# Two attention-and-mixer stages on one core: batch 2's q and k turned by DMA, w4 loaded later, work moved between engines

## The chip, the core and the metric

One core of a Trainium2 chip runs one program. The metric is device time in microseconds for one execution. Five engines work side by side, each in the order in which its instructions were written, and wait for one another through semaphores: TensorE (PE in the rows; its weight loads are PEld), VectorE (DVE), ScalarE (ACT), GpSimd (POOL) and SyncE (SP), which only issues DMA transfers. SP, POOL and ACT can each issue DMAs into a queue of their own; sixteen DMA engines serve the queues.

## The reference

For eight batches of 576 tokens with 8 heads of 64:

```python
scores = q @ k.T / 8                 # heads 0-3: keys of the last 32 tokens
attn = softmax(where(mask, scores))  # heads 4-7: every 4th key of the last 128
x = attn @ v                         # (576, 512), heads side by side
h = relu(x.T @ w_tok1) @ w_tok2      # mixes tokens
u = x + h.T
out = u + relu(u @ w_ch1) @ w_ch2    # mixes channels, 512 -> 1536 -> 512
```

Inputs and output are float32; the kernel works in float16 with float32 sums.

## The kernel before

For each batch the work has these parts, named by their tiles.
- q, k and v are loaded by SP (`emit_loads_qk`, `load_v`) and cast to float16, mostly on POOL (`cast_steps`, L275 to L286; 17 steps: the tails of q and k, then q and k of four pairs of heads, then v as four blocks `vn`, a tail `vt`, two `vd` and `vx`).
- q and k are turned, so that the 64 channels lie on partitions. For batches 0 and 1 TensorE does it against an identity (`transposes`). For batch 2 TensorE does it too (`unpad` L381, `turn_tails` L396, with copies out of PSUM on ScalarE and VectorE). For batches 3 to 7 DMA transposes issued by SP do it (`dma_steps` L348: tails, then q and k of the first two pairs, then of the last two), and POOL copies turned k into the order in which the scores read it (`place_steps` L367).
- Scores: batches 0 and 1 add the mask on TensorE as a product. Batches 2 to 7 have `scores_twin` (L509), one call for heads 0 to 3 (g = 0) and one for heads 4 to 7 (g = 1): 24 products into six PSUM banks, then six exponentials on ScalarE, then masks multiplied on POOL.
- Values (`values`), eight heads: products into a bank, then a reciprocal and a product on VectorE.
- Token mixing: `emit_h1` (rectified on VectorE or ScalarE) and `emit_u`, where u is the sum with x. For some blocks the sum is formed on TensorE by an identity product and ScalarE copies it ("summed"); for the others VectorE adds.
- u is turned (`emit_uT` by TensorE for batches 0 and 1, `uT_dma` and `uT_place` for the rest).
- Channel mixing: `gen_first` is the first layer, twelve blocks `gp` of four products with 512 columns, each rectified into `gta` (L770); for odd batches there are three more groups `gt` for the tails of two batches. `gen_second` is the second layer `yp`, which reads w4 = w_ch2; twelve products fill half an output block, and VectorE adds u.

The order of instructions is written out by `interleave` (L819): a main generator (layers of an earlier batch) yields its cost in estimated us, and steps of later batches carry a place on that scale; a step is emitted as soon as the main work has passed its place. The number is only a place in the order. The change touches the first such call, with batch 0's first layer as main work and batch 1's attention as steps (L1000 to L1005), and the second, with the first layer of batch 1 and the second layers of batches 0 and 1 as main work and the attention of batches 2 and 3 as steps (L1007 to L1024). Ahead of them stand the casts of batch 1 on POOL (L990), between which POOL issues the loads of w3's last third and of w4's three thirds.

PSUM has eight banks: three that `gp`, `gt` and `yp` take in turn ("main"), three for values, u and turning ("fl") and two for scores.

Of the kernel before, what the change touches and what calls it, by code (L numbers as in the profile page):

```python
# [69 lines left out]
def kernel(  # L70
# [201 lines left out]
    def cast_vx(b, eng):  # L272
        copy(eng, vt[b % 2][:, :, 0:64], l32[(b, "vx")])

    def cast_steps(b, eng=nc.gpsimd):  # L275
        steps = [lambda: cast_tails_qk(b, eng)]
        for hp in range(4):
            for nm in ("q", "k"):
                steps.append(lambda nm=nm, hp=hp: cast_qk(b, nm, hp, eng))
        for s in range(4):  # L280
            steps.append(lambda s=s: cast_vn(b, s, nc.gpsimd))
        steps.append(lambda: cast_tail_v(b, nc.gpsimd))
        for h in (0, 2):
            steps.append(lambda h=h: cast_vd(b, h, nc.gpsimd))
        steps.append(lambda: cast_vx(b, nc.gpsimd))
# [4 lines left out]
    gta = fixed("gt", [128, NMB, GW])  # L290
# [218 lines left out]
    def scores_twin(b, g):  # L509

        tags = (("sc", 2), ("sc", 2), ("fl", 3), ("fl", 3), ("fl", 3), ("main", 3))
        ps = [bank(*tags[i], f"sc_{b}_{g}_{i}") for i in range(6)]
        small = ps[4:6]

        def twin(hp, banks, c, keys, queries):
            for h in range(2):
                rows = slice(64 * h, 64 * h + 64)
                n = c.stop - c.start
                nc.tensor.matmul(out=banks[h][:, c], lhsT=keys(rows), rhs=queries(rows), start=True, stop=True)  # L519

        for j in range(2):
            hp = 2 * g + j
            if g == 0:
                for kb in range(3):
                    twin(hp, ps[2 * j:2 * j + 2], slice(BLK * kb, BLK * kb + BLK),
                         lambda rows: kt[hp][rows, 128 * kb:128 * kb + 128],
                         lambda rows: qta[rows, hp, :, 32 * kb:32 * kb + 40])
            else:
                for r in range(4):
                    twin(hp, ps[2 * j:2 * j + 2], slice(128 * r, 128 * r + 128),  # L530
                         lambda rows: kra[rows, hp, r], lambda rows: qta[rows, hp, r])
        for j in range(2):
            hp = 2 * g + j
            if g == 0:
                twin(hp, small, slice(256 + 128 * j, 384 + 128 * j),
                     lambda rows: kt[hp][rows, 384:512], lambda rows: qta[rows, hp, :, 96:128])
            n = 1 + g
            for x in range(n):
                c, k0 = 64 * (n * j + x), 384 + 128 * x if g else 512
                twin(hp, small, slice(c, c + 64), lambda rows: kt[hp][rows, k0:k0 + 128],  # L540
                     lambda rows: tta[rows, hp, 0:64])
        yield 0.87

        def exp(out, in_):
            nc.scalar.activation(out=out, in_=in_, func=AF.Exp, scale=0.125)  # L545

        def main(hp):
            for h in range(2):
                p = ps[2 * (hp % 2) + h]
                if g == 0:  # L550
                    exp(plain_blocks(hp)[:, h, 0:3, 0:BLK].rearrange("p b (m r) -> p b m r", r=4),
                        p[:, 0:3 * BLK].rearrange("p (b r m) -> p b m r", r=4, m=40))
                else:
                    exp(attd[hp - 2][:, h], p)

        def rest():
            for h in range(2):
                p = small[h]
                if g == 0:
                    exp(attpa[:, :, h, 3 * PST:3 * PST + 128].rearrange("p a (m r) -> p a m r", r=4),  # L560
                        p[:, 256:512].rearrange("p (a r m) -> p a m r", a=2, r=4))
                n = 1 + g
                exp(tail_cols(slice(2 * g, 2 * g + 2), g, h),
                    p[:, 0:128 * n].rearrange("p (a x c) -> p a x c", a=2, c=64))

        def mask(hp):
            if g == 0:
                w = plain_blocks(hp)[:, :, :, 0:BLK]
                mult(nc.gpsimd, w, w, band)
            else:  # L570
                w = attd[hp - 2].rearrange("p h (r c) -> p h r c", c=128)
                mult(nc.gpsimd, w, w, band[:, :, :, 0:128])
# [11 lines left out]
        mult(nc.gpsimd, t, t, tails_seen[g])  # L584
        if not g:
            mask(1)
        yield 0.0
# [30 lines left out]
    def emit_h1(b, jb, half, t):  # L618
        x = xn[b]
        j = slice(jb, DTOK, 2)  # L620
        c = slice(256 * half, 256 * half + 256)
        w = w1p if half else w1n
        p = bank("fl", 3, f"h1p_{b}_{jb}_{half}")[:, 0:256]
        nc.tensor.matmul(out=p, lhsT=w1t[b % 2][:, j], rhs=x[:, 4, c], start=True, stop=False)  # L624
        for s in range(4):
            nc.tensor.matmul(out=p, lhsT=w[:, s, j], rhs=x[:, s, c], start=False, stop=(s == 3))  # L626
        relu(nc.vector if jb and (b == 1 or (b == 0 and half)) else nc.scalar, t[:, c], p)

    def emit_u(b, s, h1):
        p = bank("fl", 3, f"up_{b}_{s}")  # L630
        if s < 4:
            summed = b == 1 and s in (0, 2)
            for half in range(2):
                c = slice(256 * half, 256 * half + 256)
                if summed:
# [110 lines left out]
    def gen_first(b):  # L746
# [17 lines left out]
        for mb in range(NMB):  # L764
            p = bank("main", 3, f"gp_{b}_{mb}")
            for i, cb in enumerate(order):
                nc.tensor.matmul(out=p, lhsT=w3_block(cb, mb), rhs=uT[(b, cb)][0], start=(i == 0), stop=(i == 3))  # L767
                if i == 1:
                    yield 0.43
            relu(nc.vector if (mb % 2 == 1 if b == 0 else mb in (1, 5)) else nc.scalar, gta[:, mb, m0:m0 + 512], p)  # L770
# [172 lines left out]
    def u_half(s, half):  # L943
        p = bank("main" if half else "fl", 3, f"up_0_{s}_{half}")[:, 0:256]
        c = slice(256 * half, 256 * half + 256)
        t = u16(0, s)[:, 2 * half:2 * half + 2]
        summed = s in (0, 2)
        if summed:
            nc.tensor.matmul(out=p, lhsT=ident, rhs=xn[0][:, s, c], start=True, stop=False)
        for jb in range(2):  # L950
# [39 lines left out]
    for i in (0, 1, 2, 3, 4, 5, 7, 6, 8, 9, 10, 11, 12, 13, 14, 15, 16):  # L990
        casts1[i]()
        if i == 1:
            load_w3(2)
        if i in (14, 15, 16):
            load_w4(next(w4s))

    def at(t0, dt, fs):
        return [(t0 + dt * i, 0.0, f) for i, f in enumerate(fs)]

    steps = score_steps(1, 0, 0, (0.0, 0.6, 0.7), (  # L1000
        (2.9, 5.0), (4.2, 6.9), (5.4, 9.3), (8.0, 12.2)))
# [69 lines left out]
```

## Time and profile before

| | us |
|---|---|
| median of three runs | 286.94 (285.69 to 287.02) |
| profiled execution | 286.81 |
| its span, first to last instruction | 285.0 |
| TensorE busy | 273.8 |
| GpSimd busy | 166.8 |
| VectorE, ScalarE busy | 132.3, 131.4 |

Times in rows count from the start of the span. A row of the timeline shows start and duration of an instruction or of a merged run of equal ones (x4), what it writes and reads, and in brackets how long its engine was idle before it and what ended that. A releaser is inferred; where several semaphores were waited for it is the last one by the profile. Matmuls overlap, so the duration of one is longer than its share of a dense run.

### The profile page before, as it was taken

Reading aid. Unit: us, or ns where it says so; the run is one execution under the profiler, and the core shown is the slowest. Engines: PE = TensorE matmul, PEld = TensorE weight load, DVE = VectorE, ACT = ScalarE, POOL = GpSimd, SP = SyncE. Lnnn points to the kernel's source line nnn. Section 1 sums busy time; section 2 is a strip of 40 time slices with the busy share of each in tenths; the row PEclk is TensorE's granted clock in tenths of the full one; section 3 lists DMA queues with packets and bytes.
Section 4 is the critical chain, followed back from the end, with each engine's and each line's share of the span. In section 5 each row is a group of like instructions: output and inputs, shape, how many; then the busy total and the mean of one; then the engine's idle time right before and its main releaser. Section 6 shows DMA issues by size and latency. Waiting matters only on the chain.

```text
span 285.0 us, 6873 instructions
## 1 busy us (share of the span) xinstructions
PE 273.8 (96%) x2760; PEld 207.0 (73%) x2760; DVE 132.3 (46%) x280; ACT 131.4 (46%) x263; POOL 166.8 (59%) x236
## 2 busy tenths in 40 slices
PE   5799899999999999999999999999999999999994
PEld 2696576676896976598776976797767966886594
DVE  6875687652365155514730263526531184322022
ACT  2964563458412374473446625482456435134500
POOL 7980853383998769769945998289945900000000
PEclk9999999999999999999999999999999999999999
DMA  7999999999658999999798989399994310521032
GB/s 217 262 227 253 269 230 241 273 223 307 165 105 191 147 332 274 190 168 352 201 191 191 319 241 188 60 235 314 207 148 83 110 39 0 111 93 37 2 86 99
DMA packets 105423, 52.60 MB, mean 185 GB/s; under 512 B 73872, under 2 KB 104208, under 8 KB 105392
## 3 DMA queue, kind: packets, MB, share of 16 engines
q1 hardware_dynamic: 101280, 47.07, 71.2%
q0 software_dynamic: 2512, 3.92, 7.6%
q10 hardware_dynamic: 1600, 1.18, 1.4%
q8 instruction: 21, 0.34, 0.5%
q14 instruction: 10, 0.08, 0.1%
HBM read 37.05 MB, written 9.44 MB: 163 GB/s over the span
## 4 chain that ended last, share of the span: by engine, by line
PE 79%; DMA 9%; POOL 4%; ACT 2%; DVE 2%; issue 1%; SPq 1%; ACTq 0%; POOLq 0%
PE gp L767 26%; PE yp L790 26%; PE h1p L626 4%; PE up L638 4%; PE gt L758 4%; PE yp L810 4%; DMA l_k<-in_k_dram 3%; DMA lt<-in_k_dram 3%; PE sc L519 2%; DMA utm<-u 2%; DMA w<-in_moe_w_tok_dram 2%; POOL attd L113 1%; PE av L605 1%; PE h1p L624 1%; PE av L600 1%
## 5 line engine op out<-in xcount | busy, mean ns | idle before, releaser
L790 PE MATMUL yp<-w,gt 128*128 128x256 f16 x756 | 86.5, 273 | 0.0
L790 PEld LDWEIGHTS <-gt 128*128 128x128 f16 x768 | 78.4, 106 | 6.2
L107 ACT ACTIVATE gt<-gp 128x512 f16<-128x512 f32 x76 | 45.4, 601 | 68.6 <-PE gp L767 68.3
L767 PE MATMUL gp<-utm,w 128*128 128x512 f16 x192 | 67.7, 379 | 0.0
L767 PE MATMUL gp<-utd,w 128*128 128x512 f16 x144 | 54.8, 380 | 0.0
L767 PEld LDWEIGHTS <-w 128*128 128x128 f16 x384 | 39.0, 114 | 20.4 <-issue 1.9
L800 DVE TENSOR_TENSOR o<-yp,u 128x512 f32<-128x512 f32 x31 | 21.4, 691 | 66.5 <-PE yp L790 64.6
L113 POOL TENSOR_TENSOR attp<-attp,const 128x1280 f16<-128x1280 f16 x12 | 31.4, 2615 | 22.4 <-ACT attp L545 18.0
L113 DVE TENSOR_TENSOR xn<-av,rec 128x320 f16<-128x320 f32 x64 | 31.5, 492 | 2.2
L113 POOL TENSOR_TENSOR attd<-attd,const 128x1024 f16<-128x1024 f16 x12 | 25.3, 2129 | 2.4 <-ACT attd L545 2.4
L644 DVE TENSOR_TENSOR u<-up,xn 128x512 f16<-128x512 f32 x26 | 17.5, 689 | 14.1 <-PE up L638 14.0
L103 POOL CAST c_k<-l_k 128x512 f16<-128x512 f32 x29 | 18.0, 623 | 8.8 <-PE tpu L675 7.6
L107 ACT ACTIVATE h<-h1p 128x256 f16<-128x256 f32 x29 | 11.1, 383 | 26.0 <-PE h1p L626 25.7
L103 POOL CAST c_q<-l_q 128x512 f16<-128x512 f32 x31 | 19.6, 635 | 2.6 <-DMA l_q<-in_q_dram 2.6
L545 ACT ACTIVATE attp<-sc 128x480 f16<-128x480 f32 (+1 forms) x36 | 16.1, 528 | 7.4 <-PE sc L519 7.4
L109 DVE TENSOR_SCALAR gt<-gp 128x512 f16<-128x512 f32 x20 | 13.7, 686 | 10.1 <-PE gp L767 10.1
L103 POOL CAST vv<-l_vn 128x256 f16<-128x256 f32 (+1 forms) x40 | 15.0, 403 | 4.0 <-DMA l_vn<-in_v_dram 3.5
L373 POOL COPY kt<-kr 128x512 f16<-128x512 f16 x10 | 10.8, 1079 | 10.4 <-DMA kr<-c_k 6.6
L697 ACT COPY utd<-utm 128x512 f16<-128x512 f16 x12 | 12.7, 1123 | 9.0 <-DMA utm<-u 9.0
L615 DVE RECIPROCAL rec<-av 128x5 f32<-128x5 f32 x64 | 12.2, 190 | 7.4 <-PE av L612 7.0
L545 ACT ACTIVATE attd<-sc 128x512 f16<-128x512 f32 x24 | 12.4, 604 | 6.1 <-PE sc L519 6.1
L758 PEld LDWEIGHTS <-w 128*128 128x128 f16 x192 | 11.9, 113 | 2.0 <-issue 0.4
(149 smaller groups left out, 441.2 us busy)
## 6 DMA issues: line engine op xcount, KB each, us to landing
out_dram<-o SPq DMA_DIRECT2D x72, 128.0 KB, 2.7
l_q<-in_q_dram SPq DMA_DIRECT2D x15, 512.0 KB, 6.9
l_k<-in_k_dram SPq DMA_DIRECT2D x14, 512.0 KB, 7.4
l_vn<-in_v_dram SPq DMA_DIRECT2D x32, 128.0 KB, 6.7
l_vd<-in_v_dram SPq DMA_DIRECT2D x16, 256.0 KB, 4.3
w<-in_moe_w_ch_dram POOLq DMA_DIRECT2D x6, 512.0 KB, 8.3
lt<-in_q_dram SPq DMA_DIRECT2D x8, 128.0 KB, 5.0
l_vt<-in_v_dram SPq DMA_DIRECT2D x8, 128.0 KB, 4.6
```

What stands on the lines that cost most here:

```text
L103: eng.tensor_copy(out=out, in_=in_)
L107: nc.scalar.activation(out=out, in_=in_, func=AF.Relu)
L109: eng.tensor_scalar_max(out=out, in0=in_, scalar1=0.0)
L113: eng.tensor_tensor(out=out, in0=x, in1=y, op=ALU.mult)
L545: nc.scalar.activation(out=out, in_=in_, func=AF.Exp, scale=0.125)
L615: nc.vector.reciprocal(out=rec[:, :, 0], in_=av[:, :, 64])
L644: nc.vector.tensor_tensor(out=u16(b, s), in0=blocks4(p), in1=blocks4(xn[b][:, s]), op=ALU.add)
L697: nc.scalar.copy(out=natural(uTd[:, cb - 2]), in_=uTm[i][:, cb].rearrange("p r m -> p m r"))
L758: nc.tensor.matmul(out=p[:, 128 * i:128 * i + 128], lhsT=w3_block(cb, 4 * g + i), rhs=uT[(b, cb)][1], start=(cb == order[0]), stop=(cb == ...
L767: nc.tensor.matmul(out=p, lhsT=w3_block(cb, mb), rhs=uT[(b, cb)][0], start=(i == 0), stop=(i == 3))
L790: nc.tensor.matmul(out=p[:, c], lhsT=gta[:, mb, a0:m0 + 512:4] if half else gta[:, mb, a0:a0 + 128], rhs=w4[mb][:, c], start=(mb == 0), st ...
L800: nc.vector.tensor_tensor(out=blocks4(o32), in0=blocks4(p), in1=u16(b, s), op=ALU.add)
```

## The change

In the first call, batch 1's scores get later places, and the turning of its q and k partly too. In the second, batch 2's q and k are turned by `dma_steps` and `place_steps` in place of `turn_steps`; its casts are emitted in two lumps, ahead of the turns and behind the placing; V of batch 2 is loaded after the turns on SP's queue; two of w4's three thirds are issued by POOL after the placing, and before the casts of V; one of these casts (the fourth `vn`) goes to ScalarE; the two twins of batch 2 stand closer together and batch 3's loads earlier. One mask of batch 2 goes from POOL to VectorE. Batch 1's h1 and part of batch 0's are rectified on ScalarE. Batch 0's first layer has one block of twelve on VectorE in place of six; the later batches have three (1, 7, 9) in place of two (1, 5). For batch 0 the u block 3 is now summed on TensorE, for batch 1 the block 0 no longer is.

```diff
-        if i in (14, 15, 16):
+        if i in (14,):
             load_w4(next(w4s))
...
-    steps = score_steps(1, 0, 0, (0.0, 0.6, 0.7), ((2.9, 5.0), (4.2, 6.9), (5.4, 9.3), (8.0, 12.2)))
+    steps = score_steps(1, 0, 0, (0.0, 0.6, 1.5), ((2.9, 5.8), (5.0, 7.7), (6.6, 9.3), (8.0, 11.4)))
-    steps += mix_steps(1, 16.0, 17.0, 18.0, 22.6, 0.6)
+    steps += mix_steps(1, 16.0, 17.0, 18.0, 30.6, 0.0)
...
-    steps = at(0, 0.0, [lambda: emit_loads_qk(2)]) + at(1.0, 0.0, [lambda: load_v(2)])
-    casts = cast_steps(2)
-    steps += at(0, 0.9, casts[:9]) + at(5.8, 0.1, casts[9:])
-    steps += turn_steps(2, (5.0, 4.8, 4.2, 6.0, 8.0, 10.3, 9.2, 12.5, 7.9, 7.0), (...))
-    steps += score_steps(2, 10.5, 4.6)
-    va = value_steps(2, 19.5, 1.2)
-    steps += mix_steps(2, 25.5, 29.0, 29.0, 37.0)
-    steps += at(13.0, 0.0, [lambda: emit_loads_qk(3)]) + at(18.0, 0.0, [lambda: load_v(3)])
-    steps += at(18.2, 0, cast_steps(3)) + at(23.0, 0.6, dma_steps(3)) + at(27.0, 0.5, place_steps(3))
-    steps += score_steps(3, 35.5, 7.0) + at(33.4, 1.5, load_steps(4))
+    steps = at(0.0, 1.5, [lambda: emit_loads_qk(2)]) + at(5.0, 6.5, [lambda: load_v(2)])
+    casts = cast_steps(2, (POOL, POOL, POOL, POOL, POOL, POOL, POOL, POOL, POOL, POOL, POOL, POOL, ACT, POOL, POOL, POOL, POOL))
+    steps += at(0.6, 0.0, casts[:9]) + at(6.5, 0.0, casts[9:])
+    steps += at(5.2, 2.5, [lambda: load_w4(next(w4s))]) + at(5.3, 1.5, [lambda: load_w4(next(w4s))])
+    steps += at(2.0, 0.5, dma_steps(2)) + at(5.1, 0.0, place_steps(2))
+    steps += score_steps(2, 10.0, 2.6)
+    va = value_steps(2, 19.0, 1.2)
+    steps += mix_steps(2, 26.6, 29.1, 30.1, 42.5)
+    steps += at(7.0, 8.0, [lambda: emit_loads_qk(3)]) + at(15.5, 0.0, [lambda: load_v(3)])
+    steps += at(17.7, 0, cast_steps(3)) + at(21.5, 1.5, dma_steps(3)) + at(27.0, 0.5, place_steps(3))
+    steps += score_steps(3, 35.0, 5.5) + at(33.4, 1.5, load_steps(4))
...
-                mult(nc.gpsimd, w, w, band)
+                mult((POOL, DVE)[hp] if b == 2 else POOL, w, w, band)
-        relu(nc.vector if jb and (b == 1 or (b == 0 and half)) else nc.scalar, t[:, c], p)
+        relu(nc.vector if jb and (b < 0) else nc.scalar, t[:, c], p)
-            relu(nc.vector if (mb % 2 == 1 if b == 0 else mb in (1, 5)) else nc.scalar, ...)
+            relu(nc.vector if mb in ((1,), (1, 7, 9), (1, 7, 9))[min(b, 2)] else nc.scalar, ...)
-            summed = b == 1 and s in (0, 2)
+            summed = b == 1 and s in (2,)
-        summed = s in (0, 2)
+        summed = s in (0, 2, 3)
```

## Rows read from the trace of the kernel before

**Rows 1.** The page: busy us of each engine, and TensorE's slices.
```profile
PE 273.8 (96%) x2760; PEld 207.0 (73%) x2760; DVE 132.3 (46%) x280; ACT 131.4 (46%) x263; POOL 166.8 (59%) x236
...
PE   5799899999999999999999999999999999999994
```
**Rows 2.** Table of stretches: busy us and instructions of each engine, clock, DMA.
```profile
30.00:40.00 10.00, 9.29 (x110) 7.06 (x111) 8.14 (x17) 6.33 (x14) 6.89 (x15) 1.00 1.21 252
```
**Rows 3.** Chain of waits, 54 to 73: start, us, what.
```profile
63.83 0.45 PE tp_q L385 x8
64.28 0.86 PE gp L767 x4
...
70.59 0.67 PE sc L519 x24
...
72.25 0.76 PE yp L790 x7
```
**Rows 4.** Groups by line and shape: busy us, mean ns of one, idle before.
```profile
L103 POOL CAST c_k<-l_k 128x512 f16<-128x512 f32 x29 | 18.0, 623 | 8.8 <-PE tpu L675 7.6 <-DMA l_k<-in_k_dram 1.1
...
L385 PE MATMUL tp_k<-const,c_k 128*128 128x128 f16 x16 | 1.5, 219 | 0.0
```
**Rows 5.** Timeline of TensorE, 28.9 to 35.2, three of its stops.
```profile
30.09 0.40 PE L310 MATMUL tp_q<-const,c_q 128*128 128x128 f16 x4 [0.50 <-POOL c_q L103]
...
32.16 0.40 PE L310 MATMUL tp_q<-const,c_q 128*128 128x128 f16 x4 [0.16 <-POOL c_q L103]
...
34.98 0.38 PE L310 MATMUL tp_k<-const,c_k 128*128 128x128 f16 x4 [0.26 <-DVE kt L103]
```
**Rows 6.** Timeline of ScalarE, one rectification.
```profile
65.18 0.60 ACT L107 ACTIVATE gt<-gp 128x512 f16<-128x512 f32 x1 [0.46 <-PE gp L767]
```
**Rows 7.** Timeline of TensorE, 54.5 to 70: stage start, twin, two stops.
```profile
54.62 3.71 PE L767 MATMUL gp<-uT,w 128*128 128x512 f16 x16
...
65.30 0.59 PE L519 MATMUL sc<-qt,kt 64*128 64x160 f16 x12
66.08 0.23 PE L519 MATMUL sc<-qt,kt 64*128 64x128 f16 x2 [0.20 <-DVE kt L103]
...
68.67 1.05 PE L758 MATMUL gt<-uT,w 128*128 128x128 f16 x16 [0.18 <-ACT attt L545]
```
**Rows 8.** DMA queues (packets, MB, share): q0 at 41 to 46, both 46 to 52, q1 65 to 69.
```profile
q0 software_dynamic: 66, 0.27, 30.4%
...
q0 software_dynamic: 286, 1.05, 86.6%
q1 hardware_dynamic: 313, 0.32, 18.5%
...
q1 hardware_dynamic: 1392, 1.37, 106.2%
```
**Rows 9.** Issue to landing: batch 2's k; w4; a block of batch 2's V at 55.
```profile
DMA to landing us min/median/max: 13.6/14.3/15.0
...
DMA to landing us min/median/max: 8.2/9.8/11.8
...
DMA to landing us min/median/max: 5.8/5.8/5.8
```
**Rows 10.** Timeline of POOL, 20 to 110: first w4 issue, one mask.
```profile
41.33 0.54 POOL L984 DMA_DIRECT2D w<-in_moe_w_ch_dram  x1 [0.19 <-issue]
...
68.54 2.60 POOL L113 TENSOR_TENSOR attp<-attp,const 128x1280 f16<-128x1280 f16 x1 [4.33 <-PE gp L767]
```
**Rows 11.** Tile kr, 83 to 93: batch 3's turns, placing, landing (min/median/max).
```profile
L351 SPq DMA_TRANSPOSE kr<-c_k x2: 1231/1248/1266, 83.9 to 87.7; - x2
L373 POOL COPY kt<-kr x2: 1055/1060/1064, 88.6 to 89.9; 128x512 f16<-128x512 f16 x2
L376 POOL COPY kt<-kr x2: 396/404/412, 91.3 to 91.6; 128x128 f16<-128x128 f16 x2
...
DMA to landing us min/median/max: 3.1/3.2/3.2
```

More of the change, by code (lines that the diff above doesn't have):

```diff
@@ L84 @@
     ps = ctx.enter_context(tc.tile_pool(name="ps", bufs=1, space=bass.MemoryType.PSUM))
+    DVE, ACT, POOL = nc.vector, nc.scalar, nc.gpsimd
     SRC = {"q": q, "k": k, "v": v}
@@ L273, in cast_vx, with cast_steps @@
         copy(eng, vt[b % 2][:, :, 0:64], l32[(b, "vx")])
-    def cast_steps(b, eng=nc.gpsimd):
-        steps = [lambda: cast_tails_qk(b, eng)]
+    def cast_steps(b, engs=(nc.gpsimd,) * 17):
+        steps = [lambda: cast_tails_qk(b, engs[0])]
         for hp in range(4):
             for nm in ("q", "k"):
-                steps.append(lambda nm=nm, hp=hp: cast_qk(b, nm, hp, eng))
+                steps.append(lambda nm=nm, hp=hp: cast_qk(b, nm, hp, engs[2 * hp + 1 + (nm == "k")]))
         for s in range(4):
[L281 to L285, printed above, removed]
+            steps.append(lambda s=s: cast_vn(b, s, engs[9 + s]))
+        steps.append(lambda: cast_tail_v(b, engs[13]))
+        for i in range(2):
+            steps.append(lambda i=i: cast_vd(b, 2 * i, engs[14 + i]))
+        steps.append(lambda: cast_vx(b, engs[16]))
         return steps
@@ L568, in mask @@
                 w = plain_blocks(hp)[:, :, :, 0:BLK]
-                mult(nc.gpsimd, w, w, band)
+                mult((POOL, DVE)[hp] if b == 2 else POOL, w, w, band)
             else:
                 w = attd[hp - 2].rearrange("p h (r c) -> p h r c", c=128)
-                mult(nc.gpsimd, w, w, band[:, :, :, 0:128])
+                mult((POOL, POOL)[hp - 2] if b == 2 else POOL, w, w, band[:, :, :, 0:128])
         main(2 * g)
@@ L583, in scores_twin @@
         t = tail_cols(slice(2 * g, 2 * g + 2), g)
-        mult(nc.gpsimd, t, t, tails_seen[g])
+        mult((POOL, POOL)[g] if b == 2 else POOL, t, t, tails_seen[g])
         if not g:
@@ L769, in gen_first @@
                     yield 0.43
-            relu(nc.vector if (mb % 2 == 1 if b == 0 else mb in (1, 5)) else nc.scalar, gta[:, mb, m0:m0 + 512], p)
+            relu(nc.vector if mb in ((1,), (1, 7, 9), (1, 7, 9))[min(b, 2)] else nc.scalar, gta[:, mb, m0:m0 + 512], p)
             yield 0.43
@@ L998, in at @@
         return [(t0 + dt * i, 0.0, f) for i, f in enumerate(fs)]
-    steps = score_steps(1, 0, 0, (0.0, 0.6, 0.7), (
-        (2.9, 5.0), (4.2, 6.9), (5.4, 9.3), (8.0, 12.2)))
+    steps = score_steps(1, 0, 0, (0.0, 0.6, 1.5), (
+        (2.9, 5.8), (5.0, 7.7), (6.6, 9.3), (8.0, 11.4)))
     va = value_steps(1, 11.3, 0.5)
     steps += va[:4] + [(p + 0.4, c, f) for p, c, f in va[4:]]
-    steps += mix_steps(1, 16.0, 17.0, 18.0, 22.6, 0.6)
+    steps += mix_steps(1, 16.0, 17.0, 18.0, 30.6, 0.0)
     interleave(gen_first(0), steps)
@@ L1010, in firsts @@
         yield from gen_second(1)
-    steps = at(0, 0.0, [lambda: emit_loads_qk(2)]) + at(1.0, 0.0, [lambda: load_v(2)])
-    casts = cast_steps(2)
-    steps += at(0, 0.9, casts[:9]) + at(5.8, 0.1, casts[9:])
-    steps += turn_steps(2, (5.0, 4.8, 4.2, 6.0, 8.0, 10.3, 9.2, 12.5, 7.9, 7.0),
-                        (nc.scalar, nc.vector, nc.scalar, nc.vector, nc.scalar, nc.vector, nc.vector, nc.vector))
-    steps += score_steps(2, 10.5, 4.6)
-    va = value_steps(2, 19.5, 1.2)
-    steps += va[:4] + [(p + 0, c, f) for p, c, f in va[4:]]
-    steps += mix_steps(2, 25.5, 29.0, 29.0, 37.0)
-    steps += at(13.0, 0.0, [lambda: emit_loads_qk(3)]) + at(18.0, 0.0, [lambda: load_v(3)])
-    steps += at(18.2, 0, cast_steps(3)) + at(23.0, 0.6, dma_steps(3)) + at(27.0, 0.5, place_steps(3))
-    steps += score_steps(3, 35.5, 7.0) + at(33.4, 1.5, load_steps(4))
+    steps = at(0.0, 1.5, [lambda: emit_loads_qk(2)]) + at(5.0, 6.5, [lambda: load_v(2)])
[5 more added lines that the diff above has]
+    va = value_steps(2, 19.0, 1.2)
+    steps += va[:4] + [(p + 0.0, c, f) for p, c, f in va[4:]]
+    steps += mix_steps(2, 26.6, 29.1, 30.1, 42.5)
+    steps += at(7.0, 8.0, [lambda: emit_loads_qk(3)]) + at(15.5, 0.0, [lambda: load_v(3)])
+    steps += at(17.7, 0, cast_steps(3)) + at(21.5, 1.5, dma_steps(3)) + at(27.0, 0.5, place_steps(3))
+    steps += score_steps(3, 35.0, 5.5) + at(33.4, 1.5, load_steps(4))
     interleave(firsts(), steps)
```

## The prediction
> **What bounds the kernel now.** First the page's busy times and slices: TensorE is busy for 273.8 of 285.0 us, and after the first slices 9 stands nearly everywhere [rows 1]. So a change of other engines' work pays only where TensorE stops. Then the table of stretches: 30 to 40 us still has a gap, 9.29 of 10 [rows 2]; the chain of waits through 63 to 73 goes from one TensorE group to the next [rows 3]; the timeline of instructions shows the stops themselves [rows 5, 7]. That is the ground that the change works on. The idle times there hide part of a stop: eight 128-column products in a row take 0.45 us, 0.056 each, though one is shown as 0.219 [rows 3, 4]. A stop therefore costs its idle time and 0.16 more.
>
> All sums are made against the profiled execution's 286.81 us (span 285.0 and 1.81 around it); the median of the runs is 286.94, 0.13 more.
>
> **Turning by DMA.** TensorE loses 16 products for k [rows 4], as many for q and 4 for the tails: 36 x 0.056 = 2.0 us, in a stretch where it is the bound. Gain 2.0. The copies out of PSUM go too, off the path.
>
> **Batch 1's scores later, rectifications on ScalarE.** At 30.09 TensorE stops for the cast of the first q, and soon after for the first k; neither the casts nor these products' place in the order move: both stops stay. The next (0.16 idle) waits for a cast too; in the new order a block of batch 0's first layer comes ahead of it, so 0.33 goes. The fourth (0.26 idle) waits for VectorE to empty a bank; VectorE loses five rectifications and the product comes later, so 0.42 goes [rows 5]. Gain 0.75. ScalarE takes five at 0.60 us [rows 6], 3.0 more over a stage of 25 us, of which it fills 6.33 in the ten that are fullest of copies and exponentials [rows 2]: hidden, and at worst a bank comes 0.6 late once. The identity products that move from batch 1's u to batch 0's (two of 256 columns each way) cost nothing, since the stop at 30.09 covers those that are added. The relu changes of the later batches lie where TensorE hardly stops: nothing, plus or minus 0.3.
>
> **The second stage up to batch 0's second layer.** Two stops go: 0.20 idle in the first twin of scores, waiting for VectorE's kt, and 0.18 ahead of the tails product, waiting for a bank of scores [rows 7]; 0.36 + 0.34 = 0.7 gained. But the two twins now stand 0.67 + 0.89 + 0.86 = 2.4 us apart (twin, sixteen products of 128 columns, one block) against 5.2 before [rows 3, 7]. ScalarE's exponentials free the last bank of the first twin 3.3 us after the twin began (65.30; the tails product that waits starts at 68.67) [rows 7]; the second twin needs that bank at 3.0, so 0.35 is lost, and about as much again for the bank behind the tails' rectification, which queues behind the exponentials. Loss 0.7. The two cancel.
>
> **The hand-over to the DMA queues.** Here is the unknown, since waits are added in queues that run in order: SyncE's turns wait for POOL's casts, POOL's placing waits for the turns, and behind these stand SyncE's V loads and POOL's two w4 loads and V casts.
> Before, from 46 to 52 us, 286 packets and 1.05 MB of w4 shared the engines with 313 packets and 0.32 MB of loads [rows 8], and k landed 13.6 and 15.0 us after issue [rows 9]. Loads alone move 1.37 MB in 4 us [rows 8]. By 46 w4 had moved 0.27 of its first third's 0.52 MB [rows 8]; at the old rate the rest is through at 47.4. The q and k then left (three loads of 0.52 less some 0.2) take 4 us: the last k lands near 52, and three casts of 0.62 later [rows 4] all is cast, near 53.9. SyncE issues the last two turns at about 53.3 and 54.7 (1.25 each, landing 3.2 after issue [rows 11]): the last k is turned at 58. POOL has placed the first two pairs by then (1.06 each, two ends of 0.40 left [rows 11]) and issues w4 at about 58.8 and 59.4.
> Who waits: stage two starts at 54.6 - 0.75 = 53.9 [rows 7]; ten blocks of 0.86 and two tails of 0.89 put the first twin at 64.3, 5 us behind the placing: covered. Batch 0's second layer starts at 64.3 + 2.4 + 0.67 + 0.86 + 0.7 = 69.0; it needs w4's second third 4 products and its last third 8 products later, 0.109 each [rows 3]: 69.4 and 69.9. Of the old w4 loads the first landed 8.2 us after issue and the slowest, with two before it, 11.8 [rows 9]: 67.0 to 71.2, so between 0 and 1.3 late. I take 0, as the last now has one before it.
> The new cast on ScalarE is narrower. It stands behind the rectification of block 6, at about 61, and waits for the fourth V load. TensorE can go on for three banks, to block 9 at 63.5; ScalarE first needs 0.7 for the cast's two parts and 0.6 for a rectification: V has to land by 62.2. SyncE issues that load at about 58.5 (behind the turns, some 0.8 each). A turn in a quiet queue lands after 3.2 [rows 11], a V load in a full one after 5.8, and k beside w4 took up to 15.0 [rows 9]. I take 4.2, near the quiet end, since q and k are through: 62.7, 0.5 late. Ends without w4 in the way: 0 and 2.1.
> The Trainium skill's page "DMA: Bandwidth & Descriptors", section "Queues, rings and completion order", states that a DMA engine takes its queues in turn, packet by packet. The 286 beside 313 packets agree. By that rule V's 256-byte packets would crawl beside w4's large ones, which is rival B.
> **Masks and the stage's end.** VectorE takes one of the four masks, 2.6 us on POOL [rows 10], and has some 9 us for it. It relieves POOL, which I count at nothing: the value products come 4.6 us into the second layer (seven halves of 0.65), 9 after the scores, and POOL needs 3.3 of these. At the end of the stage u's placing on ScalarE now stands behind the exponentials of batch 3's second twin: 3.3 us of these and a copy against 0.67 + 3.9 us of products left: 0 to 1.0 late, 0.3 taken.
>
> **Sum.** -2.0 - 0.75 - 0.7 + 0.7 + 0.5 + 0.3 = -1.95: 286.81 - 1.95 = 284.86; as a median some 0.1 more, 284.9. Its own range: 283.9 to 286.0.
>
> **Rivals.**
> A, the gain is used up by a late hand-over. If the first third of w4 holds q and k up 2 us longer, the last k is turned at 60 and V's cast and w4 slip by 2, which TensorE waits for once: 284.9 + 2.0 = 286.9, no change. For it: POOL and SyncE run this chain with no gap to catch up in. Against it: 1.05 MB less is in the way [rows 8].
> B, slower: the fourth V load meets w4. The place is ScalarE's cast; the point from which it decides is whether that load's 131 KB are through when w4's packets come in force, about 61 to 62 (2 to 3 us after issue; the first third, issued at 41.33 [rows 10], had moved 0.27 MB by 46), against 61.7 for a quiet landing. If not, 131 KB in 256-byte packets, one for each of w4's, move at a quarter of 0.32 MB per 6 us, 13 KB per us, until w4 is over 6 us on: landing near 67.5, 5.3 late instead of 0.5: 284.9 + 4.8 = 289.7. For it: k beside w4 took 15.0, in larger packets [rows 9]. Against it: V is issued before w4, and w4 starts slowly beside queued loads.
> C, nothing waits: hand-over and stage end cost 0: 284.9 - 0.8 = 284.1, and down to 283.4 where the closer twins cost nothing.
> D, the turning isn't the path: the 2.0 come back as a stop right behind, because POOL sets the pace of scores and values from 72 on: 286.9. The row of 9s that TensorE has there speaks against it, that POOL is busy for 166.8 us in all speaks for it [rows 1].
>
> **Chances.** Forecast 0.50, A 0.15, B 0.11, C 0.18, D 0.06. What a measurement tells from no change is 0.5%, 1.4 us: faster is below 285.5. That holds four fifths of the forecast (0.40) and C (0.18), 0.58; slower, above 288.4, is B and a little of A, 0.12; the rest is 0.30. The range for 8 in 10 runs from 283.0 to 288.0: it takes in C with the relus' 0.3, A and D, and leaves out B.
>
> **What would show it.** No products at the turning lines for batch 2; batch 2's k cast by 54; w4's last two issues at 59, landed by 70; the first twin at about 64.3, the second layer's first product at about 69. TensorE idle ahead of block 9 with ScalarE's cast waiting for l_vn shows B; idle at the first products of the second layer with w4 landing late shows A. The prediction is wrong if a stop of over 1 us stands anywhere after 72, where I reckon with 0.3 in all.

## The result and the profile after

The changed kernel is slower: a median of 289.51 us (288.49 to 290.12) against 286.31 (285.69 to 287.02) for the kernel before, six runs each; the ratio is 1.0106 [1.0088, 1.0124]. The forecast was 284.9, and the range ended at 288.0. The profiled execution took 289.64, its span 287.9. One of the runs below, 289.13 us of d1, was taken in a slower state of the core and is left out of the ratios.

The page, which answers to [rows 1]: TensorE has 36 products fewer, as counted, and is busy for 1.2 us less (the working had 2.0), and its slices now fall to 7 in the one that ends at 93.6 us. The DMA line had not been read ahead of the prediction.

```profile
PE 272.6 (95%) x2724; PEld 206.5 (72%) x2724; DVE 128.8 (45%) x269; ACT 130.6 (45%) x264; POOL 167.5 (58%) x239
...
PE   5899999899997999989999999999999999999993
...
DMA  8999999999988989989986989499884310520032
```

TensorE's timeline after, which answers to [rows 3, 7]. Up to the second layer all goes as the working had it: first twin at 64.92 (before 65.30; forecast 64.3), second twin 2.57 later (forecast 2.4), second layer at 69.65 (before 72.08; forecast 69.0), so 2.4 us ahead. The rest is lost at the first twins of batches 3 and 4, both times to GpSimd's copies of turned k. In the kernel before, batch 3's twin began at 91.28 with no idle time (the last line).

```profile
64.92 0.65 PE L520 MATMUL sc<-qt,kt 64*128 64x160 f16 x14
...
67.49 0.62 PE L520 MATMUL sc<-qt,kr 64*128 64x128 f16 x16
...
69.65 4.75 PE L791 MATMUL yp<-w,gt 128*128 128x256 f16 x42
...
92.55 0.38 PE L520 MATMUL sc<-qt,kt 64*128 64x160 f16 x6 [1.13 <-POOL kt L374]
93.88 0.44 PE L520 MATMUL sc<-qt,kt 64*128 64x160 f16 x8 [0.95 <-POOL kt L374]
...
121.98 0.38 PE L520 MATMUL sc<-qt,kt 64*128 64x160 f16 x6 [0.68 <-POOL kt L374]
123.31 0.44 PE L520 MATMUL sc<-qt,kt 64*128 64x160 f16 x8 [0.95 <-POOL kt L374]
```
```profile
91.28 0.65 PE L519 MATMUL sc<-qt,kt 64*128 64x160 f16 x14
```

With the part that idle time hides (0.16 to 0.17 each) these four stops cost 2.4 and 2.0 us. The last product starts at 283.2 for 281.0 before: from 2.4 us ahead to 2.2 behind is 4.6, and 4.4 of that is these stops. (Of the span's 2.9 us, 0.7 lie behind the last product; they were not followed.)

GpSimd after, which answers to [rows 10, 11]. The k casts end at 54.4, the placing at 59.2, w4 is issued at 59.12 (forecast 58.8). Then GpSimd waits 6.67 us for the tail of V and begins the masks at 71.61, where before it began at 68.54 [rows 10]. By the end of batch 3's casts it is only 0.5 us behind the kernel before (last line), since one mask fewer is its own; ahead of the placing it then waits again, for the turn.

```profile
53.81 0.62 POOL L104 CAST c_k<-l_k 128x512 f16<-128x512 f32 x1
...
59.12 1.07 POOL L985 DMA_DIRECT2D w<-in_moe_w_ch_dram  x2
60.18 1.10 POOL L104 CAST vv<-l_vn 128x256 f16<-128x256 f32 x3
67.95 0.61 POOL L104 CAST vv<-l_vt 64x512 f16<-64x512 f32 x1 [6.67 <-DMA l_vt<-in_v_dram]
...
71.61 2.60 POOL L114 TENSOR_TENSOR attp<-attp,const 128x1280 f16<-128x1280 f16 x1
...
88.75 0.40 POOL L104 CAST vt<-l_vx 128x256 f16<-128x256 f32 x1
91.45 1.04 POOL L374 COPY kt<-kr 128x512 f16<-128x512 f16 x1 [2.30 <-DMA kr<-c_k]
```
```profile
88.22 0.40 POOL L103 CAST vt<-l_vx 128x256 f16<-128x256 f32 x1
```

SyncE's queue after: start, duration of an issue, what. Batch 2's V is issued at 56.55; from 61.83 issues are slow (2.75 us for one tail load), and batch 3's two tails, two q and two k loads take until 71.26; batch 3's V follows at once, at 71.36 (its first buffers had been cast by 62.9, so it did not wait for them); the outputs and batch 3's turns stand behind that. The first k turn, issued at 88.09, holds the two pairs of heads that the first twin reads and lands some 3.2 us later, just ahead of GpSimd's copy at 91.45; the last one serves the second twin, which did not stop. Second block: the kernel before, where the same tail load took 0.61, V was issued at 64.65 and the first k turn at 83.89.

```profile
56.55 2.25 SPq L207 DMA_DIRECT2D l_vn<-in_v_dram  x4
...
61.83 2.75 SPq L196 DMA_DIRECT2D lt<-in_q_dram  x1
...
71.36 5.80 SPq L207 DMA_DIRECT2D l_vn<-in_v_dram  x4
...
88.09 1.23 SPq L352 DMA_TRANSPOSE kr<-c_k  x1
...
91.91 1.23 SPq L352 DMA_TRANSPOSE kr<-c_k  x1
```
```profile
58.80 0.61 SPq L195 DMA_DIRECT2D lt<-in_q_dram  x1
...
64.65 5.39 SPq L206 DMA_DIRECT2D l_vn<-in_v_dram  x4
...
83.89 1.27 SPq L351 DMA_TRANSPOSE kr<-c_k  x1
```

Batch 4's stops have the same form: its first k turn is issued at 117.39 (115.09 before), and GpSimd, free at 118.14, waits 2.74 us for it.

The DMA queues after (packets, MB, share of 16 engines), which answer to [rows 8]: at 60 to 62, and at 62 to 64, when w4 has come in force.

```profile
q0 software_dynamic: 25, 0.10, 35.1%
q1 hardware_dynamic: 623, 0.15, 34.7%
...
q0 software_dynamic: 96, 0.39, 99.5%
q1 hardware_dynamic: 77, 0.02, 7.6%
```

Packet for packet, V's 256 bytes beside w4's 4096: V gets 0.02 MB in 2 us. The rule of the Trainium skill that the prediction weighed (page "DMA: Bandwidth & Descriptors", section "Queues, rings and completion order", queues served in turn by packets) fits these two counts. How many packets of each queue make up a turn they do not show.

### The profile page after: what moved, and what is told of

Same layout as the page of the kernel before. It is cut to its first block, busy times and chain, and to the rows that moved or that the text cites. A ratio compares the mean times of both kernels' runs of the same rounds, so it can differ in the third digit from the quotient of the medians.

```text
span 287.9 us, 6800 instructions
## 1 busy us (share of the span) xinstructions
PE 272.6 (95%) x2724; PEld 206.5 (72%) x2724; DVE 128.8 (45%) x269; ACT 130.6 (45%) x264; POOL 167.5 (58%) x239
## 4 chain that ended last, share of the span: by engine, by line
PE 65%; DMA 17%; POOL 8%; SPq 4%; issue 2%; DVE 2%; ACT 1%; POOLq 0%
PE yp L791 24%; PE gp L768 19%; DMA l_vn<-in_v_dram 5%; DMA l_vx<-in_v_dram 4%; DMA kr<-c_k 3%; DMA l_k<-in_k_dram 3%; PE h1p L627 3%; PE gt L759 3%; PE yp L811 3%; SPq L207 3%; PE up L639 2%; PE sc L520 2%; POOL vv L104 2%; DMA const<-consts 2%; POOL attd L114 1%
## 5 line engine op out<-in xcount | busy, mean ns | idle before, releaser
L108 ACT ACTIVATE gt<-gp 128x512 f16<-128x512 f32 x74 | 44.4, 601 | 71.0 <-PE gp L768 70.5
L114 POOL TENSOR_TENSOR attp<-attp,const 128x1280 f16<-128x1280 f16 x11 | 28.8, 2617 | 18.1 <-ACT attp L546 18.0
L110 DVE TENSOR_SCALAR gt<-gp 128x512 f16<-128x512 f32 x22 | 15.1, 688 | 30.2 <-PE gp L768 30.2
L108 ACT ACTIVATE h<-h1p 128x256 f16<-128x256 f32 x32 | 12.3, 384 | 24.6 <-PE h1p L627 23.9
L374 POOL COPY kt<-kr 128x512 f16<-128x512 f16 x12 | 12.8, 1067 | 11.9 <-DMA kr<-c_k 9.6
L645 DVE TENSOR_TENSOR u<-up,xn 128x512 f16<-128x512 f32 x27 | 18.1, 687 | 1.3 <-PE up L639 0.8
L104 POOL CAST vv<-l_vn 128x256 f16<-128x256 f32 (+1 forms) x38 | 14.4, 408 | 4.4 <-DMA l_vn<-in_v_dram 3.8
```

Source lines behind the costliest of these rows:

```text
L104: eng.tensor_copy(out=out, in_=in_)
L108: nc.scalar.activation(out=out, in_=in_, func=AF.Relu)
L110: eng.tensor_scalar_max(out=out, in0=in_, scalar1=0.0)
L114: eng.tensor_tensor(out=out, in0=x, in1=y, op=ALU.mult)
L374: nc.gpsimd.tensor_copy(out=natural(kt[hp][:, 0:512]), in_=kra[:, hp].rearrange("p r m -> p m r"))
L645: nc.vector.tensor_tensor(out=u16(b, s), in0=blocks4(p), in1=blocks4(xn[b][:, s]), op=ALU.add)
```

## Experiments

Two theories follow from this profile. (In the expectations below, "V's buffers" and "late V casts" as what holds SyncE up are the theory of the time; the queue shown above did not wait for them.) Theory 1: w4's late loads keep V and SyncE's queue back, and from there GpSimd and batch 3's turned k. Theory 2, first form: only the places of batch 3's turns, interleaved with outputs, make them late. The kernel before, in each group of runs, had a median of 286.24 to 286.40.

**First group: places, order, and the first stage alone.**

```diff
-at(21.5, 1.5, dma_steps(3))
+at(21.5, 0.2, dma_steps(3))          # a1_turns_dense
```


> The changed kernel with batch 3's five DMA turns emitted close together (from 21.5 on, 0.2 apart, not 1.5), so that SyncE no longer issues output stores between them. Theory 1 (SyncE's queue as a whole runs late, because V of batch 2 stands behind the turns and w4 keeps the DMA engines busy from 60 to 68 us): SyncE still comes to the first of these turns at about 83 us, the first k is turned some 2 us earlier than the 91.4 of the changed kernel, the stop ahead of batch 3's first twin shrinks from 2.4 to about 0.5, but SyncE stays late for batch 4 and about half of the second stop (2.0) is left: 286.5. Theory 2 (the places of these turns alone do it): both stops go, 285.0. If neither: 289.5.

289.84, ratio 1.011 [1.0065, 1.0154]. Batch 3's first k turn was issued at 86.62 (88.09 in the changed kernel), its last at 89.36, and the stop at its twin shrank to 0.3 idle, but a stop of 1.00 came at batch 2's values (GpSimd's masks) and batch 4's stops were 0.84 and 0.95 (0.68 and 0.95). The places alone are not the cause: theory 2 falls in that form.

```diff
-        if i in (14,):
+        if i in (14, 15, 16):            # a2_w4_early: all of w4 as before
-    steps += at(5.2, 2.5, [lambda: load_w4(...)]) + at(5.3, 1.5, [lambda: load_w4(...)])
```


> The changed kernel with all three thirds of w4 loaded early again, between the casts of batch 1, so that nothing stands behind the placing but V's casts. Theory 1: V of batch 2 lands by 64 and not 71, batch 3's loads end some 5 us earlier on SyncE's queue, its turns begin at 80.7 and not 83.1; both stops shrink, to 1 us each: 287. Theory 2: the turn of the first k stays behind the same output store, which waits for TensorE, so it is issued at 88 as before and both stops stay: 289.5. Cost in either case: k of batch 2 lands near 57, placed near 62, still ahead of its scores at 65.

290.59, ratio 1.0135 [1.0101, 1.0168]. Here rival B's place shows. ScalarE's cast waits for the fourth V load, the rectifications behind it hold TensorE's banks, and no stop is left later, since TensorE itself is late. First ScalarE, then TensorE:

```profile
66.81 0.83 ACT L102 CAST vv<-l_vn 128x256 f16<-128x256 f32 x2 [5.17 <-DMA l_vn<-in_v_dram]
```
```profile
68.31 1.25 PE L768 MATMUL gp<-uT,w 128*128 128x512 f16 x4 [4.69 <-ACT gt L108]
```

V was late here not for w4's packets but because k landed later, so the turns and the V loads behind them on SyncE's queue were issued later (V at 61.09).

```diff
-at(5.0, 6.5, [lambda: load_v(2)])
+at(1.0, 6.5, [lambda: load_v(2)])    # a3_v_first: V ahead of the turns
```


> The changed kernel with V of batch 2 issued by SyncE ahead of the turns, as before the change. Theory 1: V no longer meets w4, POOL's V casts end near 62 and not 71.6, SyncE's batch 3 loads begin earlier; against it the turns of batch 2 come behind V's 1.3 MB, so k is placed near 62 and w4's last two loads are issued near 62, landing near 70: a stop of 1 at the second layer; in sum about 288. Theory 2: as the changed kernel, 289.5, plus that stop.

290.82, ratio 1.0156 [1.0116, 1.0195]. V is in time, but the last k turn is issued 3.6 us later (58.79), w4 at 64.52, and the second layer waits for it twice:

```profile
72.64 1.01 PE L791 MATMUL yp<-w,gt 128*128 128x256 f16 x4 [3.45 <-DMA w<-in_moe_w_ch_dram]
75.55 2.72 PE L791 MATMUL yp<-w,gt 128*128 128x256 f16 x12 [1.89 <-DMA w<-in_moe_w_ch_dram]
```

The kernel before with only the edits of the first call (the summed blocks too):

```diff
-    steps = score_steps(1, 0, 0, (0.0, 0.6, 0.7), ((2.9, 5.0), (4.2, 6.9), ...))   # a4_first_stage
+    steps = score_steps(1, 0, 0, (0.0, 0.6, 1.5), ((2.9, 5.8), (5.0, 7.7), ...))
-        relu(nc.vector if jb and (b == 1 or (b == 0 and half)) else nc.scalar, t[:, c], p)
+        relu(nc.scalar, t[:, c], p)
-            relu(nc.vector if (mb % 2 == 1 if b == 0 else mb in (1, 5)) else nc.scalar, ...)
+            relu(nc.vector if mb in ((1,), (1, 5), (1, 5))[min(b, 2)] else nc.scalar, ...)
```

> The kernel before with only the edits of the first stage: batch 1's scores later, batch 0's rectifications and both batches' h1 on ScalarE, the identity sums moved. By the prediction's step two stops go and 0.75 is gained: 285.6 against 286.3 for the kernel before. Rival: from 60 us on SyncE and POOL set the pace (batch 3's scores started the moment POOL had placed k at 91.3 in the kernel before), so TensorE gives the gain back there: 286.3.

285.71 (12 runs), ratio 0.9972 [0.9949, 0.9995]: 0.7 us, the 0.75 of the working, kept to the end. This version beats both kernels, the kernel before only just: the interval ends at 0.9995.

**Second group: which part of the hand-over.**

```diff
-    w4 = [w4a[:, i] for i in range(NMB)]
+    w4 = [w4a[:, i % 4] for i in range(NMB)]    # c1_one_w4; the two late loads are left out
```


> The changed kernel without its two late w4 loads; the second layers read w4's first third three times (so two thirds of w4 are left out). Theory 1 (w4's late loads hold up batch 2's V, and through V's casts and V's buffers GpSimd's masks and SyncE's queue): the last V cast ends near 64 in place of 71.6, batch 2's masks start near 68.3, batch 3's turned k is placed from about 87, no stop above 0.6 us after 72; time 289.5 - 4.4 - 0.5 = 284.6. Theory 2 (the pace: GpSimd works without a gap from batch 2's masks to batch 3's placing, and SyncE nearly so, and what TensorE gained ahead of that comes back as stops whatever V does): stops of about 2 us stay at batch 3's first twin, time 287 to 288.

284.87 (284.16 to 285.39), ratio 0.9953 [0.9936, 0.9971]. The second layers read w4's first third three times, so this kernel leaves out the other two. With w4's late loads gone and all else of the change in place, the time is the forecast. V's last cast ends at 67.1 (expected 64), the masks begin at 68.04, SyncE issues batch 3's tails, q and k in 5.0 us (61.69 to 66.68; 9.4 in the changed kernel) and its first k turn at 82.70, and batch 3's twin starts at 90.31 with nothing to wait for. One stop of 0.92 stays at batch 4's twin, against the expected "no stop above 0.6 us after 72". GpSimd, SyncE, then TensorE:

```profile
68.04 2.61 POOL L114 TENSOR_TENSOR attp<-attp,const 128x1280 f16<-128x1280 f16 x1 [0.92 <-ACT attp L546]
...
87.01 1.08 POOL L374 COPY kt<-kr 128x512 f16<-128x512 f16 x1 [0.87 <-PE up L639]
```
```profile
82.70 1.23 SPq L352 DMA_TRANSPOSE kr<-c_k  x1
```
```profile
90.31 0.65 PE L520 MATMUL sc<-qt,kt 64*128 64x160 f16 x14
...
119.08 0.44 PE L520 MATMUL sc<-qt,kt 64*128 64x160 f16 x8 [0.92 <-POOL kt L374]
```

The kernel a2 with the fourth V cast back on GpSimd:

```diff
-    casts = cast_steps(2, (..., POOL, ACT, POOL, POOL, POOL, POOL))    # c2_w4_early_vpool
+    casts = cast_steps(2, (..., POOL, POOL, POOL, POOL, POOL, POOL))
```

> The changed kernel with w4 loaded early, as before, and the fourth V cast back on GpSimd. If the stop of 4.9 us at 63 in the kernel with w4 early was ScalarE's cast waiting for V, it goes, and the first twin is near 65. V is issued at 61 here, 4.5 later than in the changed kernel, because k lands later: its casts end near 70.5, only 1 us ahead of the changed kernel's. Theory 1 in the form that any late V costs the same: stops of 1.5 to 2.4 us at batch 3's first twin and some at batch 4's, time 287.5 to 289. Theory 1 in the form that only w4's packets in SyncE's queue cost: stops below 1 us, time 285 to 286.

288.95, ratio 1.0092 [1.0071, 1.0113]. The stop of 4.7 goes and the first twin is at 64.68, which shows that ScalarE's cast was its cause. But k is placed so late that this twin stops for 0.88, V is issued at 63.6, the masks begin at 73.64, and stops come at the values (1.58), at batch 3's twin (0.39 and 0.95) and at batch 4's (0.95). So k and V that are late through SyncE's order cost about as much as V that is late through w4; with w4 loaded early as before, the rest of the change does not pay either.

Each late third as four loads of one row in four, packets of 1 KB:

```diff
-            out=w4a[:, 4 * i:4 * i + 4], in_=w)
+        for j in range(4 if i else 1): ... out=w4a[:, 4 * i + j], in_=w[:, j]    # c3_w4_quarters
```

> The changed kernel with each of the two late w4 loads as four loads of a quarter, so packets of 1 KB in place of 4 KB. If the DMA engines take packets of the two queues in turn, V gets about four times the share: the V tail lands near 64 in place of 67.9, V's casts end near 66, the stops at batch 3's and 4's twins shrink to under 1 us each; w4 lands later, by 71 to 72, a stop of 0 to 1.5 us at the start of the second layer. Time 285.5 to 287.5. If V is held up by something else than the packets' size, all stays: 289.5.

290.56, ratio 1.0159 [1.0111, 1.0206]: not expected. The packets do alternate, 661 of w4 beside 740 at 66 to 70, and V's tail is cast at 64.0 in place of 67.95. But the engine time of a byte is no lower (0.895 of 16 engines for 4 us over 661 packets is 0.087 us for 1 KB; 0.995 for 2 us over 96 was 0.33 for 4 KB), so what V's first loads gain w4 loses: the second layer waits for it three times, until 72.17 (0.26, 0.62 and 0.87 idle), the last V load is as late as it was, its cast over at 71.9, and batch 3's twin stops for 1.67 and 0.95. The eight issues also take GpSimd 4.25 us in place of 1.07 for two, so this run changes more than the packets.

```profile
q0 software_dynamic: 661, 0.60, 89.5%
q1 hardware_dynamic: 740, 0.20, 32.8%
```

Batch 3's V loads behind its turns, its V casts behind the placing:

```diff
-at(15.5, 0.0, [lambda: load_v(3)]), at(17.7, 0, cast_steps(3))
+at(28.1, 0.0, [lambda: load_v(3)]), at(17.7, 0, casts[:9]) + at(31.0, 0, casts[9:])   # c4_v3_behind_turns
```

> The changed kernel with batch 3's V loads moved behind batch 3's turns on SyncE's queue, and its V casts behind the placing on GpSimd. Theory 1 (SyncE's queue is late because batch 3's V loads wait for batch 2's late V casts and stand ahead of the turns): batch 3's last k turn is issued near 83 in place of 91.9, GpSimd places it by 90 without a wait, no stop over 0.5 at batch 3's first twin (2.4 us gained); the 9.5 us of V issues then stand ahead of batch 4's loads, so the stops at batch 4's twin stay or grow to 4 us; time 287 to 290. Theory 2 (GpSimd's pace): the 4 us of V casts that leave GpSimd's chain would help too, so here it expects the same at batch 3's twin; but GpSimd would have no idle time ahead of the placing.

290.86, ratio 1.0158 [1.0122, 1.0194]. Batch 3's twin starts at 91.08 without a stop, as both theories had it, with the first k turn at 85.39 in place of 88.09, though the last came only at 89.28: outputs and late casts stood ahead of it, not V alone. The V issues then hold up the transposes of u, and the stop is at the next stage's start:

```profile
104.81 0.38 PE L768 MATMUL gp<-utd,w 128*128 128x512 f16 x1 [3.24 <-ACT utd L698]
```

**Third group: how much w4, and w4 without the turning.** Late loads are cut to one, the last third left out (d1) or the middle third loaded early (d2); the kernel before loads two thirds a second time (d3); and a4 gets batch 2's mask and the rectifications 7 and 9 on VectorE (d4).

```diff
-    steps += at(5.2, 2.5, [lambda: load_w4(...)]) + at(5.3, 1.5, [lambda: load_w4(...)])
+    steps += at(5.2, 2.5, [lambda: load_w4(...)])                # d1_two_w4, d2_middle_early
+    w4 = [w4a[:, i if i < 8 else i - 4] for i in range(NMB)]     # d1
+        if i in (14, 15):                                        # d2
+    steps += at(4.0, 0.0, [lambda: load_w4(1), lambda: load_w4(2)])   # d3_before_w4_again
+                mult((nc.gpsimd, nc.vector)[hp] if b == 2 else nc.gpsimd, w, w, band)   # d4_first_and_mask
```

> The changed kernel with one late w4 load in place of two; the second layers read w4's second third in place of its last (a third of w4 is left out). Theory 1 (the late w4 loads take the DMA engines from batch 2's V and from SyncE's queue): half the bytes cost about half: V's last cast near 69, a stop of about 1 us at batch 3's first twin, time 286 to 287.5, between 284.9 without a late load and 289.5 with two. Rival (any late load pushes V over the edge, the size does not matter): 289.

286.97 (284.78 to 289.13, 12 runs), ratio 1.001 [0.9987, 1.0034]: between none (284.87) and two (289.51). V's last cast ends at 69.4, batch 3's stops are 2.2 us in all. The run also tells SyncE from GpSimd: GpSimd's casts ahead of the placing end at 86.91, earlier than in the kernel before (88.62), and it still waits 2.85 us for the first k turn, issued at 86.40. The stop comes by SyncE's queue.

```profile
89.76 1.04 POOL L374 COPY kt<-kr 128x512 f16<-128x512 f16 x1 [2.85 <-DMA kr<-c_k]
```

> The changed kernel with w4's middle third loaded early and only the last late; nothing is left out. Theory 1: behind the hand-over as with one late load, but q and k land 2 to 3 us later, so turns, V's loads and w4 start that much later: time 287 to 289, above that of the kernel with one late load and no early one.

288.95, ratio 1.0082 [1.0053, 1.011]: as expected in size, but the stop is elsewhere, 2.43 idle in the first layer, where ScalarE is idle for 2.91 ahead of its cast; the profile's releaser is GpSimd's third V cast, which had itself waited 1.52 for its load.

> The kernel before, turning on TensorE, with w4's last two thirds loaded a second time at about 56 us on GpSimd's queue. Theory 1 (w4's bytes there suffice): V's last cast at 67 to 69 in place of 63.6, masks about where they were, batch 3's q, k and V loads 5 us later, SyncE's 6 us of slack ahead of batch 3's turns used up, a stop of 0.5 to 1.5 us at batch 3's first twin: time 287 to 288. Rival (only together with the turning, which adds bytes and holds V back on SyncE's queue): the slack takes it, time within 0.5 of 286.4.

290.14, ratio 1.0131 [1.01, 1.0163], more than expected. w4's bytes hold V back without any DMA turning: GpSimd waits 5.22 us for the fourth V block, and behind that cast stands batch 2's last q cast, which TensorE needs for turning. The slack at batch 3's turns was never reached.

```profile
63.98 0.87 POOL L103 CAST vv<-l_vn 128x256 f16<-128x256 f32 x2 [5.22 <-DMA l_vn<-in_v_dram]
```
```profile
66.84 0.61 PE L385 MATMUL tp_q<-const,c_q 128*128 128x128 f16 x4 [3.43 <-POOL c_q L103]
```

> The kernel before with the first-stage edits, and with batch 2's mask on VectorE and the later batches' rectifications (1, 7, 9) on VectorE: everything of the change but the DMA turning, w4 and the places of the second stage. Theory 1: no stop in the later stages to remove, so the same as the first-stage edits alone, 285.7, give or take 0.4. Rival (GpSimd's chain from batch 2's masks to batch 3's placing sets the pace): 2.6 us less on it give up to 1 us more: 284.7.

287.81, ratio 1.0063 [1.0037, 1.009]: both expectations fall. The mask takes VectorE 3.27 us, and the copy of turned k stands behind it, so the second twin waits. The length is not the mask's own: the same instruction took 0.83 us where GpSimd was not masking at the time (e1, third block), and 3.27 in all four runs in which GpSimd's mask of 2.60 had begun 0.01 to 0.02 us before it (a2, c1, e2 and this one). In c1 and e2 it was 3.27 too, and no product waited for it, since there the DMA queues had taken the copies away.

```profile
67.88 3.27 DVE L113 TENSOR_TENSOR attp<-attp,const 128x1280 f16<-128x1280 f16 x1 [2.16 <-ACT attp L545]
```
```profile
71.55 0.40 PE L519 MATMUL sc<-qt,kr 64*128 64x128 f16 x8 [1.26 <-DVE kr L103]
```
```profile
67.30 0.83 DVE L114 TENSOR_TENSOR attp<-attp,const 128x1280 f16<-128x1280 f16 x1 [2.46 <-ACT attp L546]
```

**Fourth group: order or bytes.** Every byte is kept; w4 is issued behind three V casts (e1), or behind the V tail's too (e2).

```diff
-    steps += at(0.6, 0.0, casts[:9]) + at(6.5, 0.0, casts[9:])
+    steps += at(0.6, 0.0, casts[:9]) + at(5.15, 0.0, casts[9:12]) + at(6.5, 0.0, casts[12:])   # e1; e2 adds casts[13]
```


> The changed kernel with GpSimd's casts of the first three V blocks ahead of the two late w4 loads, so w4 is issued near 61.3 in place of 59.1; same bytes, nothing left out. Order theory (V stands behind w4, and only that costs): V's last cast near 67 to 68 in place of 71.6, batch 2's masks from 68.5, no stop above 1 us at batch 3's first twin; w4 lands near 70.5, a stop of 0 to 1 us at the start of the second layer; time 285 to 286.5. Bytes theory (w4, V and batch 3's loads together are more than the DMA engines move before they are needed, so that each order is late somewhere): a stop of 1.5 to 3 us at the second layer's start or the same stops at batch 3's twin, time 288 to 290.

288.80, ratio 1.0102 [1.0076, 1.0127]. In this run w4 was issued at 59.80 (its placing ended 1 us sooner), and only the last V load was caught: GpSimd waits 6.86 for it, the masks begin at 70.87, and batch 3's stops are 1.41 and 0.95.

> The same with V's tail cast ahead of w4 too: w4 issued near 64. Order theory: V's last cast near 67, masks on time, but w4 lands near 72, 2 us late: a stop of 2 to 2.5 us at the second layer's start and none at batch 3's twin; time 286.5 to 287.5. Bytes theory: 289 to 291.

289.75, ratio 1.0122 [1.0086, 1.0158]. w4 is issued at 63.00, V's casts end at 65.7 and the masks begin at 67.15, as the order theory had it, with no stop at batch 3's twin and one where w4 is late. The time is that of the bytes theory all the same (the traced execution is the fastest of the six, 288.17). First e2, then the same products in e1:

```profile
72.09 5.35 PE L791 MATMUL yp<-w,gt 128*128 128x256 f16 x34 [2.42 <-DMA w<-in_moe_w_ch_dram]
```
```profile
70.39 3.87 PE L791 MATMUL yp<-w,gt 128*128 128x256 f16 x34 [0.58 <-DMA w<-in_moe_w_ch_dram]
```

Behind the stop of 2.42 the 34 products take 5.35 us in place of 3.87: the granted clock of 70 to 76 is 0.72, so 1.5 us more go to the lower level. And SyncE, with w4 now beside batch 3's loads, issues the first k turn at 86.19 and the last at 90.55, for 83.89 and 87.72 in the kernel before; no stop follows only because TensorE is late itself. Each order of w4 and V that was tried is late somewhere, which speaks for the bytes.

## Why the prediction was wrong

**What held.** The turning products, the first stage (0.75 forecast, 0.7 measured alone; in the profiled execution the second stage starts only 0.3 earlier, at 54.31 for 54.62), the k casts by 54.4, w4 issued at 59.1, landing 5.8 and 9.1 us after issue and in time for 69.65, the fourth V block cast on ScalarE at 62.04 with no wait, the first twin and the second layer 0.6 us later than said. Leaving out the late loads gives 284.87 against the forecast of 284.9, so the rest of the sum stood, at least as a whole. That the two agree to 0.03 is in part luck: the forecast was counted from 286.94, the median of three runs, where more runs gave 286.3, so the gain was 1.4 us and not 2.0, and a stop at batch 4's twin that the sum did not have is in it (0.92 idle).

**The step that failed** is "The hand-over to the DMA queues", in its part "Who waits". It followed two readers of the late transfers, the second layer (w4) and ScalarE's cast (the fourth V load), and priced the hand-over at 0.5. It named what stands behind, "SyncE's V loads and POOL's two w4 loads and V casts", and did not follow it on. The V loads five to eight land after w4 has come in force, and GpSimd's masks, behind their casts, begin 3.1 us late (71.61 for 68.54). Behind V on SyncE's queue stand batch 3's tails, q and k, which the working left out: beside w4 their six issues take 9.4 us, against 5.0 without w4's late loads (c1) and 4.2 with w4 loaded early (a2). What stands behind these is late in turn: batch 3's V loads (71.36 for 64.65), the outputs, and the first k turn (88.09 for 83.89), for which the placing and the first twin wait. In place of 0.5 the hand-over cost 4.4 us, in the four stops at the twins of batches 3 and 4.

Of the two ways to the stop it was SyncE's that carried it: GpSimd was free at 89.15, 0.5 later than in the kernel before, and waited 2.30 for the turn; in d1 it was free earlier than before and waited 2.85. That GpSimd's relief of one mask was counted at nothing was wrong, though: without the 2.6 us of that mask it would have come to the placing some 3 us late itself (an estimate from these rows).

**The argument behind it** was "1.05 MB less is in the way" of q and k. That is true until 54, but the bytes come back. The tables of stretches show it; first before, then after (last columns: clock, DMA share, GB/s):

```profile
52.00:64.00 12.00, 11.59 (x113) 8.05 (x111) 6.26 (x11) 6.29 (x11) 7.96 (x16) 1.00 1.10 253
...
76.00:82.00 6.00, 6.00 (x83) 5.72 (x82) 4.56 (x12) 0.00 (x0) 6.00 (x8) 1.00 0.35 105
```
```profile
52.00:64.00 12.00, 11.59 (x93) 7.31 (x92) 3.88 (x7) 7.08 (x13) 7.32 (x14) 1.00 0.89 181
...
76.00:82.00 6.00, 5.71 (x74) 5.30 (x72) 4.44 (x12) 0.00 (x0) 6.00 (x7) 1.00 0.97 229
```

Before, the DMA engines were full (1.10; the share counts overlapping packets) from 52 to 64 and largely idle (0.35) at 76 to 82. After, they run at 0.89 while SyncE's queue waits for casts to turn, and the work that was not done then is done later, when 0.97 stands where 0.35 stood.

**The rivals.** B, "the fourth V load meets w4", had V's packets beside w4's, and a chance of 0.11; its place was wrong, since the fourth load was through and the next four were not, and that its price (289.7, for one wait of ScalarE's cast) came near the measured 289.51 is luck. A stop at that place came only where V was issued later still (a2 and d2). D, GpSimd's pace from 72 on, is true of the stretch but decides little by itself: with V in time the gain is kept but for one stop at batch 4's twin (c1). The sentence that a stop of over 1 us after 72 would make the prediction wrong was the right test.

**What stays open.** Whether some order of all of batch 2's and batch 3's loads fits w4 in: every one that was tried was late somewhere, which is not a proof. The spread of d1 (284.8 to 288.5 without the run of 289.13) was not explained. c1 takes away w4's bytes and their order at once. Why SyncE's issues are slow beside w4 was not tested: that the DMA engines are busy is not enough, since in a2 the six issues took 4.2 us at a DMA share of 1.22, and in the changed kernel 9.4 at 1.10.

## What to carry to other kernels

Read the DMA line of the page as one reads TensorE's: where it stands at 9 over the whole stretch of a change, moving a load later moves the lateness, not the bytes. When a wait is added in an in-order queue, follow everything behind it until it meets a row with slack, the loads of the next batch and the time that it takes to issue them included; here that was some 30 us away, by SyncE's queue and GpSimd's copies. And see which of two late inputs came last: both GpSimd and SyncE were late here, and only SyncE set the stop. Leaving the disputed transfer out is the cheapest experiment of all: it separated a sum that was right from one term that was not.

## What the runs showed of the hardware

Packets of a quarter of the size gave the other queue more turns, but no lower engine time a byte (0.087 us for 1 KB, 0.33 for 4 KB), and the last V load landed no sooner. Issuing can be slow beside another queue's large packets: one tail load took SyncE 2.75 us to issue beside w4, and 0.61 in the kernel before. The same mask took VectorE 0.83 us by itself and 3.27 when GpSimd's mask of 2.60 had begun just before it. A stop on TensorE can cost more than its idle time: 2.42 us were followed by 1.5 more at the lower clock (0.72 granted over 70 to 76 in e2), and two stops of 0.84 and 0.95 by a granted clock of 0.75 over 120 to 126 (a1), while the two stops of 1.13 and 0.95 in the changed kernel left the granted clock at 1.00.
